# A gated mix of a state-space convolution and an MLP on one core: the front's written order from a re-fitted plan, log dt loaded with the other parameters, the skip term loaded on GpSimd's queue

## The chip, the cores and the metric

One core of one Trainium2 chip. The metric is the device time of one execution in microseconds (us). The kernel before has a median of 525.67 us over 3 runs (524.36 to 526.06). One further execution was profiled; it took 527.21 us, and its span from the first to the last instruction is 525.4 us.

## The reference

Two branches read the same input x (2048 rows by 512 columns, float32), and a gate of each row mixes them:

```python
x = A_u
g = _sigmoid((x * gate_w).sum(-1, keepdims=True))
a = _A_ref(x, A_re, A_im, B_re, B_im, C_re, C_im, log_dt, Dskip)
b = _B_ref(x, w1, b1, w2, b2)          # gelu(x @ w1 + b1) @ w2 + b2, 512 -> 1792 -> 512
return g * a + (1 - g) * b
```

The first branch builds, for each of the 512 channels, a kernel of 2048 taps from 128 complex states, and convolves the channel with it; it then adds the skip term:

```python
P = jnp.exp(logdA[:, :, None] * l[None, None, :])      # logdA = exp(log_dt) * (A_re + i A_im)
K = jnp.einsum("dn,dnl,dn->dl", Cc, P, dB).real
y = irfft(rfft(u, 2L) * rfft(K, 2L))[:L] + u * Dskip
```

## The kernel before, in words

The kernel has two parts. `front` makes the taps, the first stage of the transforms of taps and signal, and nearly all of the MLP. `conv` does the rest of the transforms, the last MLP products and the mix. In the profile, the front fills TensorE until 412.35 us, and the first matmul of `conv` starts at 416.61 us.

**The MLP in the front.** The hidden layer is cut into 64 steps `i`: 16 blocks `b` (8 blocks of 256 rows, each passed twice, with one half of the 1792 hidden columns per pass) times 4 column groups `j`. Every float32 product is made of three matmuls, of a rounded high part and a rest: `xh`, `xlo` for x, `wh`, `wl` for the weights, `hh`, `hl` for the hidden values. A step is `hidden` (L950 to L952, 12 matmuls for each of one or two column tiles, into one of three PSUM buffers `ph`), a gelu and a rounded copy on ScalarE (L967, L970), the rest `hl` on VectorE (L980), and `output` (L998 to L1000, into `acc0` and `acc1`). After j = 3 ScalarE scales `acc` by the gate into `io` (L1019), which SyncE stores in the first pass and GpSimd's queue adds to the output in HBM in the second (L1030).

**The weights.** All of the first half of w1 and w2 is loaded at the start (L1044, 14 loads of 256 KB on SyncE's queue), rounded by ScalarE (`wh`, L828; a few on VectorE, L826) and subtracted on VectorE (`wl`, L830). TensorE runs 13 matmuls on a zeroed tile `dm` before the first weights come (L1055).

**The taps.** 16 chunks, four to each of 4 units of 128 channels. A chunk makes complex powers on VectorE (`cmul`, L534 to L537), magnitudes (L691) and rotations (L703, L710, L714) into `y`, and contracts them over the 128 states on TensorE (`contract`, L728, 128 small matmuls into `pk`). After each second chunk a first stage of the transform follows (`first_stage`, L435, into `ph`, `pk`, `pu0`, `pu1`); ScalarE copies it to `sk` (L754). After each unit, eight transfers on SyncE's queue store `sk` to HBM (`tk_d`, L769). The step sizes dt = exp(log dt) are made once for unit 0 (`first_dt`: an own load of 64 KB, log dt broadcast over the partitions, L515; ten VectorE operations L490 to L503, one Exp L507), and for the other units in `other_dts`. Unit 0's parameters come in another load (`prm`, L556).

**The signal.** In 8 stages, two 128-row tiles of x are loaded (L449) and taken through a first stage (L435). ScalarE copies the four PSUM buffers to three rotating buffers `st` (L453), and two transfers each store them to HBM (`tu_d`, L456). With three buffers for four copies, the fourth copy of a stage (out of `pu1`) waits until the first buffer's two stores have landed.

**What sets the order.** Nothing is written out by hand. Each operation of the front is added to a `Plan` with an engine, an assumed duration (`hold`, in `vec`, `act`, `mm`, `move`), what it reads and writes, and a due time worked out of a table of constants (`T_0`, `LAG`, `D_LO` and so on). `Plan.run` is a small list scheduler: again and again it takes the engine that can start first, and on it the ready operation with the least due time (plus `TABLE` where ScalarE would have to load another function table). Transfers are held to share one wire, and the time of a transfer is its size over a rate of 360 KB per us. The instructions are then issued in the order that comes out, and every engine works its own list strictly in that order. So the constants and the assumed durations act on the chip only through the order. In `conv` the order is written in loops.

Of the kernel before, what the change touches and what calls it, by code (L numbers as in the profile page):

```python
# [32 lines left out]
NB = 2 * NSB  # L33
T_0 = 21.909
T_MLP = 406.545
K_0 = 31.523
T_KG = 356.763
U_0 = 28
U_GAP = 18
LAG = 12.856  # L40
TABLE = 19.14
D_KA = -33.555
D_KP = -84.187
D_S1 = 23.678
D_EV = -33.402
D_H = -65.365
D_LO = -21.589
PS = (2, 3, 1, 2)
N_ACC, N_H, N_PK, N_PU = PS
D_SP = 2.869  # L50
MEM = (6, 2, 3)
N_LD, N_HL, N_ST = MEM
D_XS = -168.313
D_G = 1.725
N_WARM = 13
T_EARLY, T_LOFT, T_DEN = 405.144, 330.334, 535.529
Y_K, Y_U = 43.23, 26.971
W_MLP = (-0.0644, -0.031, 0.0179)
W_KG = (-0.0422, -0.0319, -0.0259)
W_U = (-0.0349, -0.1398, -0.0169)  # L60
D_MAG = -0.166
D_ROT = 0.588
D_CON = 0.043
D_PHA = 0.289
D_PRE = -2.671
D_XL = 25
D_COE = -3.439
D_OUT = -2.679
N_REST = 3
D_KA0 = 0  # L70
D_DT = 19
D_PRM = -248.822
D_D0 = -601.022
D_WAVE0 = -266.408
D_COE0 = -24.094
D_SP1 = -464.705
D_G0 = 1
D_GW = 522.519
D_XS0 = 74.778
T_PRE = 0  # L80
W_CAST = (0, 0, 0, 0, 0, 0, 0, 0, 1, 1, 0, 1, 0, 0)
X_CAST = (1, 0, 1, 0)
D_X0, D_B2, D_B2C = -1509.465, -139.804, -674.499
B_CAST = 1
# [110 lines left out]
LANES = 8  # L195
TURN_PE = 0.095


# [21 lines left out]
class Plan:  # L220
# [26 lines left out]
    def run(self, fixed=None):  # L247
# [13 lines left out]
        for _ in self.tasks:  # L261
# [44 lines left out]
def gated_mix(  # L306
# [6 lines left out]
    logdt: bass.AP,  # L313
    logdt0: bass.AP,
    dskip: bass.AP,
# [33 lines left out]
    def front(pool, psum, keep, attic, loft, den):  # L349
# [133 lines left out]

        def make_dt(x, k, r, ki, key, due, load, store):
# [20 lines left out]
            move(180 if n < UW else 84, load, due - 1, [], [key], hold=0.65 if n < UW else 0.4)  # L505
            vec(4 * (n + 130), before, due, [], [key])
            act(n, lambda: nc.scalar.activation(r, r, AF.Exp, scale=0.25), due, [], [key], table="exp")  # L507
            vec(6 * (n + 130), behind, due, [], [key] if store is r else [key, "dtb"])

        def first_dt():  # L510

            x, k, r, ki = (loft[:, 2048 + UW * m : 2048 + UW * m + UW] for m in range(4))
            make_dt(
                x, k, r, ki.bitcast(I32), "tt", D_D0,
                lambda: nc.sync.dma_start(x, logdt0), dtb,  # L515
            )

        def other_dts():

            x, k, r, ki = dts  # L520
            shape = "o (p c) -> (o p) c"
            make_dt(
                x, k, r, ki.bitcast(I32), "dt", D_DT,
                lambda: nc.sync.dma_start(x, logdt.rearrange(shape, c=4)), r,
            )
            move(180, lambda: nc.sync.dma_start(dt_d.rearrange(shape, c=4), r), D_DT, ["dt"], ["dt_d"], out=True, hold=0.65)

# [23 lines left out]
        def prepare(u, t, eb_k):  # L551
# [3 lines left out]
            act_due = t + D_KA + (0 if u else D_KA0)  # L555
            move(393, lambda: nc.sync.dma_start(pr, prm[u]), t - 20 if u else D_PRM, [], ["pr"])  # L556
            if u:
                move(
                    66, lambda: nc.gpsimd.dma_start(dtb, dt_d[:, sl].to_broadcast([P, UW])), t - 20,
                    ["dt_d"], ["dtb"], queue="GP",  # L560
                )
# [86 lines left out]
        def waves(t):  # L648
# [4 lines left out]

            act(99 * CW, sines, t + D_KA, ["ph"], ["tt"], "sin", ops=3)

# [62 lines left out]
        def contract(u, c, k, t):  # L718
# [45 lines left out]
            for h in range(8):  # L764
# [8 lines left out]

                move(448, store, t + 5, [("sk", i, j) for i in range(2) for j in range(4)], [], out=True, hold=0.65)

# [92 lines left out]
        def dots(b, t):  # L868

            for n in range(2 * b, 2 * b + 2):  # L870
                xd, key = load(xs[n], t - 10)
                vec(
                    512,
                    lambda n=n, xd=xd: nc.vector.scalar_tensor_tensor(
                        xd, xd, 1.0, gwb, ALU.mult, ALU.mult, accum_out=gs[:, n : n + 1]
                    ),
                    t, ["gwb"], [key, ("gs", n // 2)],
                )

        def gates(b0, b1_, t):  # L880
# [11 lines left out]
            )  # L892
            vec(100, sides, t + D_LO, [], keys)

# [45 lines left out]
        def hidden(i, t):  # L940
# [24 lines left out]
            def gelu():  # L965
# [18 lines left out]
        def output(i, t):  # L984
# [19 lines left out]
            for s in range(2):  # L1004
                if b == NB - 1 or i == 4 * NB - 6:
# [5 lines left out]
                mm(  # L1011
                    0.2295 * n, lambda s=s, q=q: products(s, acc[q]), t + LAG + D_OUT * (j == 3),
                    [hk, lk, "b2", *ws], [("acc", q)], lat=0.45,
# [20 lines left out]
        def dense():  # L1034
# [304 lines left out]
_NAMES = [  # L1339
    "xl", "xs", "xt", "prm", "logdt", "logdt0", "dskip", "w1", "b1", "w2", "b2", "gw", "c1", "g1", "c2",  # L1340
]


def layout(inputs):
# [11 lines left out]
    names = ["A_A_re", "A_A_im", "A_B_re", "A_B_im", "A_C_re", "A_C_im"]  # L1356
    prm = np.stack([np.asarray(inputs[n])[order].T for n in names], 1)
    prm = prm.reshape(P, 6, D // UW, UW).transpose(2, 0, 1, 3)
    w1 = np.asarray(inputs["B_w1"]).reshape(4, P, NF, P).transpose(2, 1, 0, 3).reshape(NF, P, D)
# [6 lines left out]
        "logdt": np.asarray(inputs["A_log_dt"])[order].reshape(1, D),  # L1366
        "logdt0": np.broadcast_to(np.asarray(inputs["A_log_dt"])[order][:UW], (P, UW)),
        "dskip": np.asarray(inputs["A_Dskip"])[order].reshape(16, 4, 8).transpose(1, 0, 2).reshape(4, P),
# [34 lines left out]
```

## Time and profile before

| what | value |
|---|---|
| median of 3 runs | 525.67 us (524.36 to 526.06) |
| profiled execution | 527.21 us, span 525.4 us |
| mean granted TensorE clock | 0.986 |
| TensorE busy | 504.2 us (96%) |
| VectorE busy | 428.7 us (82%) |
| ScalarE busy | 351.5 us (67%) |
| GpSimd busy | 42.1 us (8%) |
| moved by DMA | 107.87 MB, 205 GB/s on average |

The busy time of TensorE is an upper bound of its work, since matmuls overlap; where the engine waits is better read from the idle time before single matmuls. A row of the chain of waits gives the start, the length and the engine with its tile and line; "SPq" is SyncE's queue, and "ACT L967" without a tile is the load of a function table. Times in the table of stages are those of one stretch, and "PEclk" is the granted TensorE clock in it.

### The profile page before, as it was taken

How to read it: one execution, taken by the hardware profiler on the slowest of the kernel's cores; microseconds unless marked ns; L12 is line 12 of the kernel's file. 1: busy time of each engine (PE TensorE's matmuls, PEld its weight loads, DVE VectorE, ACT ScalarE, POOL GpSimd, SP SyncE). 2: the span in 40 equal slices, each digit the busy share in tenths (PEclk: the TensorE clock that was granted, in tenths of full speed). 3: DMA queues.
4: the chain of work that ended last, by engine and by line, in shares of the span. 5: the costliest groups of instructions: out<-in, count | busy, mean ns of one | idle time of the engine just before them, and what ended most of it. 6: DMA issues, size and time to landing. Idle time of an engine off the chain costs nothing.

```text
span 525.4 us, 12205 instructions
## 1 busy us (share of the span) xinstructions
PE 504.2 (96%) x4810; PEld 387.0 (74%) x4810; DVE 428.7 (82%) x793; ACT 351.5 (67%) x626; POOL 42.1 (8%) x81
## 2 busy tenths in 40 slices
PE   6999998999999999999999999899999699999995
PEld 6897887799888989888898887778889542222451
DVE  6899989999999997979999899599931177777643
ACT  5798754899884789885686996556644346565311
POOL 2000000000000000002000020001010000110113
PEclk8899999999999999999999999999999899999999
DMA  8867784251684233538462267782388978999978
GB/s 293 327 226 235 262 297 145 81 203 51 186 223 141 81 110 125 193 128 192 91 203 42 81 161 198 165 301 42 113 234 197 291 252 319 354 346 388 343 285 310
DMA packets 80128, 107.87 MB, mean 205 GB/s; under 512 B 39396, under 2 KB 40680, under 8 KB 79528
## 3 DMA queue, kind: packets, MB, share of 16 engines
q1 hardware_dynamic: 74056, 85.10, 50.1%
q0 software_dynamic: 5088, 18.59, 13.3%
q10 hardware_dynamic: 928, 3.41, 1.8%
q8 instruction: 38, 0.62, 0.5%
q14 instruction: 18, 0.15, 0.1%
HBM read 61.46 MB, written 45.62 MB: 204 GB/s over the span
## 4 chain that ended last, share of the span: by engine, by line
PE 72%; ACT 8%; DMA 8%; DVE 8%; SPq 2%; issue 1%; ACTq 0%; DVEq 0%
PE pk L728 9%; PE ph L950 7%; PE ph L952 7%; PE ph L951 7%; PE acc L998 7%; PE acc L999 6%; PE acc L1000 6%; PE p2u L1160 6%; PE p2k L1160 6%; PE pa L1199 3%; DMA tu_d<-attic 3%; PE pb L1304 3%; PE ph L435 2%; DMA attic<-in_xs_dram 2%; SPq L769 2%; ACT ph L967 2%
## 5 line engine op out<-in xcount | busy, mean ns | idle before, releaser
L950 PE MATMUL ph<-xh,wh 128*128 128x256 f32 x448 | 129.2, 288 | 2.2 <-ACT wh L828 2.0
L952 PE MATMUL ph<-xh,wl 128*128 128x256 f32 x448 | 128.2, 286 | 1.2 <-DVE wl L830 1.2
L951 PE MATMUL ph<-xlo,wh 128*128 128x256 f32 x448 | 127.9, 286 | 0.0
L950 PEld LDWEIGHTS ph<-xh,wh 128*128 128x128 f32 x448 | 86.4, 193 | 9.9 <-issue 5.4
L951 PEld LDWEIGHTS ph<-xlo,wh 128*128 128x128 f32 x448 | 86.5, 193 | 2.1
L952 PEld LDWEIGHTS ph<-xh,wl 128*128 128x128 f32 x448 | 86.5, 193 | 1.4 <-DVE wl L830 1.4
L998 PE MATMUL acc<-wh,hh 128*128 128x512 f32 x206 | 82.8, 402 | 2.3 <-ACT hh L970 2.3
L1000 PE MATMUL acc<-wh,hl 128*128 128x512 f32 x206 | 80.9, 393 | 0.5 <-DVE hl L980 0.5
L999 PE MATMUL acc<-wl,hh 128*128 128x512 f32 x206 | 80.9, 393 | 0.0
L967 ACT ACTIVATE ph<-ph,b1t 128x256 f32<-128x256 f32 x112 | 50.4, 450 | 43.2 <-PE ph L952 41.3
L728 PE MATMUL pk<-y,den 128*32 128x64 f32 x2048 | 61.6, 290 | 1.2 <-DVE y L714 1.2
L728 PEld LDWEIGHTS pk<-y,den 128*32 128x32 f32 x2048 | 57.2, 136 | 5.5 <-issue 3.5
L980 DVE TENSOR_TENSOR hl<-ph,hh 128x512 fp32r<-128x512 f32 (+1 forms) x62 | 38.2, 618 | 25.3 <-ACT hh L970 24.9
L998 PEld LDWEIGHTS acc<-wh,hh 128*128 128x128 f32 x206 | 38.7, 188 | 17.5 <-issue 7.2
L691 DVE TENSOR_TENSOR y<-y,ea 128x64 f32<-128x64 f32 (+4 forms) x80 | 45.3, 566 | 3.5 <-ACT y L681 3.0
L1000 PEld LDWEIGHTS acc<-wh,hl 128*128 128x128 f32 x206 | 38.7, 188 | 10.3 <-DVE hl L980 1.6
L999 PEld LDWEIGHTS acc<-wl,hh 128*128 128x128 f32 x206 | 38.7, 188 | 6.3
L534 DVE TENSOR_TENSOR loft<-den,zz 128x256 f32<-128x256 f32 (+2 forms) x48 | 37.3, 777 | 1.1 <-ACT den L660 0.6
L970 ACT CAST hh<-ph 128x512 fp32r<-128x512 f32 (+1 forms) x62 | 33.0, 533 | 7.3 <-PE acc L999 5.5
L1168 ACT COPY k<-p2k 128x512 f32<-128x512 f32 x32 | 18.8, 586 | 28.6 <-issue 13.1
L535 DVE TENSOR_TENSOR loft<-den,zz 128x256 f32<-128x256 f32 (+2 forms) x48 | 37.1, 773 | 0.0
L703 DVE TENSOR_TENSOR y<-y,loft 128x2048 f32<-128x2048 f32 x16 | 36.6, 2285 | 0.0
(193 smaller groups left out, 880.1 us busy)
## 6 DMA issues: line engine op xcount, KB each, us to landing
tu_d<-attic SPq DMA_DIRECT2D x64, 128.0 KB, 3.5
tk_d<-sk SPq DMA_DIRECT2D x32, 256.0 KB, 4.9
t_d<-sa SPq DMA_DIRECT2D x32, 256.0 KB, 5.1
tk<-tk_d SPq DMA_DIRECT2D x24, 256.0 KB, 4.9
t<-t_d POOLq DMA_DIRECT2D x9, 512.0 KB, 6.4
attic<-in_xt_dram SPq DMA_DIRECT2D x16, 256.0 KB, 4.5
attic<-in_xs_dram SPq DMA_DIRECT2D x16, 256.0 KB, 4.9
xh_d<-xh SPq DMA_DIRECT2D x8, 512.0 KB, 3.8
```

The lines of the kernel that those rows point to most:

```text
L534: vec(2 * m, lambda: vv.tensor_mul(t, a, br), due, [ka, *kb], [kt])
L691: nc.vector.tensor_mul(both(n, 64 - 3 * n, n), both(0, 64 - n, n), an)
L728: nc.tensor.matmul(pks[q][32 * j : 32 * j + 32, :, gg], x[:, r, :, ch], y[:, r, :, ch], start=(r == 0), stop=(r == 1), skip_group_check=True,)
L950: nc.tensor.matmul(p, h, xh[xk][:, d], start=(d == 0), stop=False)
L951: nc.tensor.matmul(p, h, xlo[xk][:, d], start=False, stop=False)
L952: nc.tensor.matmul(p, lo, xh[xk][:, d], start=False, stop=(d == 3))
L967: nc.scalar.activation(phs[q][:, n], phs[q][:, n], AF.Gelu_apprx_tanh, bias=b1t[:, f : f + 1])
L980: nc.vector.tensor_sub(lo, phs[q][:, 0:nf], hi.bitcast(F32))
L998: nc.tensor.matmul(a, h, wh[1][w], start=start, stop=False)
L999: nc.tensor.matmul(a, h, wl[1][w], start=False, stop=False)
L1000: nc.tensor.matmul(a, l, wh[1][w], start=False, stop=(j == 3))
L1160: nc.tensor.matmul(out[64 * i : 64 * i + 64], w, x, start=True, stop=True)
```

## The change

Five things are changed, and lines after the first of them move by one to four.

1. **The planner's costs.** In `Plan.run` every transfer that starts after 22 us takes 1.18 times as long on the wire. The ScalarE cost of the gelu step and of the sines, and the VectorE cost of the gate's products, are raised; the broadcast of dt counts 300 KB where it counted 66 KB. Nearly all due times have new values, and the output products of the block before the last get an offset of their own (`D_LAST`).
2. **log dt beside the parameters.** The tile `pr` has seven slices where it had six, and the seventh is what was the tile `dtb`. For unit 0 one load brings all seven (448 KB); the load of 64 KB and its input are gone. Units 1 to 3 load six slices, and GpSimd's queue loads dt into the seventh, as before.
3. **The skip term.** Its load of 2 KB into `dm` moves from SyncE's queue to GpSimd's.
4. **Both halves of the first x block** are rounded by ScalarE (`X_CAST`); one was rounded by VectorE.
5. **The order** that follows from the plan.

```diff
-T_0 = 21.909
-T_MLP = 406.545
+T_0 = 22.399
+T_MLP = 408.145
...
-LAG = 12.856
-TABLE = 19.14
+LAG = 14.812
+TABLE = 27.405
...
+D_LAST = -1.557
...
-X_CAST = (1, 0, 1, 0)
+X_CAST = (0, 0, 1, 0)
...
+SLOW = 1.18
...
-                wire = max(wire, at + before) + took
+                wire = max(wire, at + before) + took * (SLOW if at > 22.0 else 1.0)
...
-        pr = pool.tile([P, 6, UW], F32, name="pr")
-        dtb = pool.tile([P, UW], F32, name="dtb")
+        pr = pool.tile([P, 7, UW], F32, name="pr")
+        dtb = pr[:, 6]
...
-            x, k, r, ki = (loft[:, 2048 + UW * m : 2048 + UW * m + UW] for m in range(4))
-            make_dt(
-                x, k, r, ki.bitcast(I32), "tt", D_D0,
-                lambda: nc.sync.dma_start(x, logdt0), dtb,
-            )
+            k, r, ki = (loft[:, 2048 + UW * m : 2048 + UW * m + UW] for m in range(3))
+            move(459, lambda: nc.sync.dma_start(pr, prm[0]), D_PRM, [], ["pr", "dtb"])
+            make_dt(dtb, k, r, ki.bitcast(I32), ["tt", "dtb"], D_D0, dtb)
...
-            move(393, lambda: nc.sync.dma_start(pr, prm[u]), t - 20 if u else D_PRM, [], ["pr"])
             if u:
+                move(393, lambda: nc.sync.dma_start(pr[:, 0:6], prm[u, :, 0:6]), t - 20, [], ["pr"])
...
-                ops=nf + 2,
+                ops=nf + 3.3,
...
-                    mm(0.2295 * n, ..., t + LAG + D_OUT * (j == 3),
+                    mm(0.2295 * n, ..., t + LAG + D_OUT * (j == 3) + D_LAST * (b == NB - 2) * j,
...
-            move(20, lambda: nc.sync.dma_start(dm[0:P:32], dskip), -80, [], ["dm"], hold=0.65)
+            pl.add("GP", 0.7, lambda: nc.gpsimd.dma_start(dm[0:P:32], dskip), D_DM, [], ["dm"], wire=(0.2, (2.2, 9.0)))
```

The order moves on every engine, while the number and the shapes of the operations stay the same but for the load and the cast named. Three places matter below.

**VectorE, at the start.** Before, from the second half of x's rest (`xlo`) on; L498 to L503 are the second part of dt's chain, and `wl00` is the first weight tile's rest, without which the first column tile's third matmul can't run:

```order
L830 TENSOR_TENSOR xlo00_108<-attic_76,xh00_106 128x512
L498 TENSOR_TENSOR loft_77<-loft_77 128x128
L499 TENSOR_TENSOR loft_77<-loft_77 128x128
L500 TENSOR_SCALAR loft_77<-loft_77 128x128
L501 TENSOR_SCALAR loft_77<-loft_77 128x128
L502 CAST loft_77<-loft_77 128x128
L503 TENSOR_TENSOR dtb_101<-loft_77 128x128
L830 TENSOR_TENSOR wl00_124<-sk_93,wh00_110 128x512
```

The same place now:

```order
L826 TENSOR_TENSOR xlo00_107<-attic_76,xh00_105 128x512 x2
L491 TENSOR_SCALAR loft_77<-pr_100 128x128
L492 TENSOR_SCALAR loft_77<-loft_77 128x128
L493 SCALAR_TENSOR_TENSOR loft_77<-loft_77,pr_100 128x128
L494 SCALAR_TENSOR_TENSOR loft_77<-loft_77 128x128
L826 TENSOR_TENSOR wl00_123<-sk_93,wh00_109 128x512
L499 TENSOR_TENSOR loft_77<-loft_77 128x128
```

Both halves of `xlo` now stand ahead of the whole dt chain, and `wl00` stands between its first four and its last six operations. On ScalarE the Exp of that chain (L507) stood ahead of the first weight cast (`wh00`), and now stands behind it.

**ScalarE, at the eighth and last signal stage** (near 337 us in the profile). Before, from the scaled outputs of a block on; L650 to L652 are the sines of the next chunk of taps, L453 the fourth copy of the signal stage, L967 and L970 gelu and rounded copy of a hidden step, L660 and L681 copies that the next chunk needs:

```order
L1019 ACTIVATE io0_144<-acc0_85,gate_69 128x512
L1019 ACTIVATE io1_145<-acc1_86,gate_69 128x512
L650 ACTIVATE loft_77<-phase_95 128x1056
L651 ACT_TABLE_LOAD
L651 ACTIVATE loft_77<-phase_95 128x1056
L652 ACTIVATE loft_77<-loft_77,half_pi_64 128x1056
L453 COPY attic_76<-pu1_92 128x512
L967 ACT_TABLE_LOAD
L967 ACTIVATE ph1_88<-ph1_88,b1t_68 128x256 x2
L970 CAST hh1_139<-ph1_88 128x512
L660 COPY den_78<-x4_97 128x2x128
L681 COPY y_94<-ea1_99 128x32
```

The same place now (L646 to L648 are the sines, L454 the copy, L963 and L966 gelu and copy, L677 and L656 the chunk's copies):

```order
L1016 ACTIVATE io0_143<-acc0_85,gate_69 128x512
L1016 ACTIVATE io1_144<-acc1_86,gate_69 128x512
L646 ACTIVATE loft_77<-phase_95 128x1056
L647 ACT_TABLE_LOAD
L647 ACTIVATE loft_77<-phase_95 128x1056
L648 ACTIVATE loft_77<-loft_77,half_pi_64 128x1056
L963 ACT_TABLE_LOAD
L963 ACTIVATE ph1_88<-ph1_88,b1t_68 128x256 x2
L966 CAST hh1_138<-ph1_88 128x512
L454 COPY attic_76<-pu1_92 128x512
L677 COPY y_94<-ea1_99 128x32
L656 COPY den_78<-x4_97 128x2x128
```

The fourth copy has moved behind the gelu and the rounded copy of `hh1`. It still stands ahead of the two copies for the next chunk. At the second and the sixth stage it has moved behind a gelu in the same way, at the third behind sines, and at the fourth behind the next chunk's copies.

**ScalarE, at the last first stage of the taps** (394 us in the profile). Before; L746 is a copy of the contraction, L754 are the four copies to `sk`:

```order
L967 ACTIVATE ph0_87<-ph0_87,b1t_68 128x256 x2
L970 CAST hh1_139<-ph0_87 128x512
L746 COPY s11_105<-pk0_90 128x512
L967 ACTIVATE ph1_88<-ph1_88,b1t_68 128x256 x2
L970 CAST hh2_140<-ph1_88 128x512
L754 COPY sk_93<-ph0_87 128x64x8
L754 COPY sk_93<-pk0_90 128x64x8
L754 COPY sk_93<-pu0_91 128x64x8
L754 COPY sk_93<-pu1_92 128x64x8
L967 ACTIVATE ph2_89<-ph2_89,b1t_68 128x256
L970 CAST hh1_139<-ph2_89 128x256
```

The same place now:

```order
L742 COPY s11_104<-pk0_90 128x512
L963 ACTIVATE ph0_87<-ph0_87,b1t_68 128x256 x2
L966 CAST hh1_138<-ph0_87 128x512
L750 COPY sk_93<-ph2_89 128x64x8
L750 COPY sk_93<-pk0_90 128x64x8
L750 COPY sk_93<-pu0_91 128x64x8
L750 COPY sk_93<-pu1_92 128x64x8
L963 ACTIVATE ph1_88<-ph1_88,b1t_68 128x256 x2
L966 CAST hh2_139<-ph1_88 128x512
L963 ACTIVATE ph2_89<-ph2_89,b1t_68 128x256
L966 CAST hh1_138<-ph2_89 128x256
```

One hidden step of two column tiles (`ph1`, 24 matmuls on TensorE) stood ahead of the four copies and now stands behind them. On TensorE, between the last matmul of that first stage and the first matmul of `conv`, there were 96 hidden and 30 output matmuls, and now there are 120 and 30. On SyncE's queue, between the last eight stores to `tk_d` and the constants and taps that `conv` loads first, there were two loads of the signal, and now there are three.

More of the change, by code (lines that the diff above doesn't have):

```diff
@@ L33 @@
 NB = 2 * NSB
-T_0 = 21.909
-T_MLP = 406.545
-K_0 = 31.523
-T_KG = 356.763
-U_0 = 28
-U_GAP = 18
-LAG = 12.856
-TABLE = 19.14
[L42 to L47, printed above, removed]
+T_0 = 22.399
+T_MLP = 408.145
+K_0 = 32.114
+T_KG = 351.806
+U_0 = 29
+U_GAP = 18
+LAG = 14.812
+TABLE = 27.405
+D_KA = -32.407
+D_KP = -80.929
+D_S1 = 7.912
+D_EV = -40.921
+D_H = -80.673
+D_LO = -23.342
 PS = (2, 3, 1, 2)
 N_ACC, N_H, N_PK, N_PU = PS
-D_SP = 2.869
+D_SP = -0.52
 MEM = (6, 2, 3)
 N_LD, N_HL, N_ST = MEM
-D_XS = -168.313
-D_G = 1.725
+D_XS = -157.526
+D_G = 1.227
 N_WARM = 13
-T_EARLY, T_LOFT, T_DEN = 405.144, 330.334, 535.529
-Y_K, Y_U = 43.23, 26.971
+T_EARLY, T_LOFT, T_DEN = 353.026, 381.686, 484.328
+Y_K, Y_U = 44.535, 26.725
 W_MLP = (-0.0644, -0.031, 0.0179)
[L59 to L68, printed above, removed]
+W_KG = (-0.0372, -0.0319, -0.0262)
+W_U = (-0.0347, -0.139, -0.0186)
+D_MAG = -0.783
+D_ROT = 0.578
+D_CON = 0.705
+D_PHA = 0.305
+D_PRE = -3.087
+D_XL = 34
+D_COE = -3.192
+D_OUT = -3.305
+D_LAST = -1.557
 N_REST = 3
 D_KA0 = 0
[L71 to L79, printed above, removed]
+D_DT = 5
+D_PRM = -277.043
+D_D0 = -1024.07
+D_WAVE0 = -343.734
+D_COE0 = -66.219
+D_SP1 = -461.8
+D_G0 = 2
+D_GW = 598.738
+D_XS0 = 98.527
 T_PRE = 0
 W_CAST = (0, 0, 0, 0, 0, 0, 0, 0, 1, 1, 0, 1, 0, 0)
-X_CAST = (1, 0, 1, 0)
-D_X0, D_B2, D_B2C = -1509.465, -139.804, -674.499
+X_CAST = (0, 0, 1, 0)
+D_X0, D_B2, D_B2C, D_DM = -1313.069, -235.635, -950.754, -4.033
 B_CAST = 1
@@ L481, in early, with make_dt @@
             yield None
-        def make_dt(x, k, r, ki, key, due, load, store):
+        def make_dt(x, k, r, ki, keys, due, store):
             ln2h = 355.0 / 512.0
@@ L503, in behind @@
                 v.tensor_mul(store, r, ki.bitcast(F32))
[L505 to L508, printed above, removed]
+            vec(4 * (n + 130), before, due, [], keys)
+            act(n, lambda: nc.scalar.activation(r, r, AF.Exp, scale=0.25), due, [], keys[:1], table="exp")
+            vec(6 * (n + 130), behind, due, [], keys)
         def first_dt():
-            x, k, r, ki = (loft[:, 2048 + UW * m : 2048 + UW * m + UW] for m in range(4))
-            make_dt(
-                x, k, r, ki.bitcast(I32), "tt", D_D0,
-                lambda: nc.sync.dma_start(x, logdt0), dtb,
-            )
+            k, r, ki = (loft[:, 2048 + UW * m : 2048 + UW * m + UW] for m in range(3))
+            move(459, lambda: nc.sync.dma_start(pr, prm[0]), D_PRM, [], ["pr", "dtb"])
+            make_dt(dtb, k, r, ki.bitcast(I32), ["tt", "dtb"], D_D0, dtb)
         def other_dts():
@@ L772, in store @@
                     )
-                move(448, store, t + 5, [("sk", i, j) for i in range(2) for j in range(4)], [], out=True, hold=0.65)
+                move(450, store, t + 5, [("sk", i, j) for i in range(2) for j in range(4)], [], out=True, hold=0.65)
         def taps():
@@ L1011, in output @@
                 mm(
-                    0.2295 * n, lambda s=s, q=q: products(s, acc[q]), t + LAG + D_OUT * (j == 3),
+                    0.2295 * n, lambda s=s, q=q: products(s, acc[q]),
+                    t + LAG + D_OUT * (j == 3) + D_LAST * (b == NB - 2) * j,
                     [hk, lk, "b2", *ws], [("acc", q)], lat=0.45,
@@ L1356, in layout @@
     names = ["A_A_re", "A_A_im", "A_B_re", "A_B_im", "A_C_re", "A_C_im"]
-    prm = np.stack([np.asarray(inputs[n])[order].T for n in names], 1)
-    prm = prm.reshape(P, 6, D // UW, UW).transpose(2, 0, 1, 3)
+    prm = [np.asarray(inputs[n])[order].T for n in names]
+    prm.append(np.broadcast_to(np.asarray(inputs["A_log_dt"])[order], (P, D)))
+    prm = np.stack(prm, 1).reshape(P, 7, D // UW, UW).transpose(2, 0, 1, 3)
     w1 = np.asarray(inputs["B_w1"]).reshape(4, P, NF, P).transpose(2, 1, 0, 3).reshape(NF, P, D)
```

18 lines of the change are left out of this document (7 added, 11 removed).

## The prediction

> **What bounds the kernel now.** I read the stages first, with the busy time of each engine in them. The first number of a row is its length; then come TensorE, its weight loads, VectorE, ScalarE and GpSimd, the granted clock, the share of DMA, and GB/s.
>
> ```profile
> 20.90:385.10 364.20, 357.13 (x3914) 307.69 (x3912) 339.92 (x642) 278.74 (x493) 22.20 (x46) 1.00 0.55 162
> 385.10:412.40 27.30, 27.25 (x301) 24.50 (x299) 3.37 (x6) 11.86 (x25) 2.46 (x3) 1.00 0.83 179
> 412.40:421.90 9.50, 5.29 (x13) 3.00 (x15) 1.12 (x2) 2.81 (x7) 0.00 (x0) 0.64 1.02 358
> ```
>
> TensorE has work nearly all the time, so a new order can only win back what TensorE waits, and what it does at half clock. From 20.9 to 385.1 us VectorE is busy for 339.92 of 364.20 us as well (93%). So the two are bound together there: what VectorE loses soon reaches TensorE. Then the waits of TensorE (total, times, longest):
>
> ```profile
> PE p2k L1160 <- DMA tk<-tk_d: 4.3, 1, 4.3
> PE acc L998 <- ACT hh L970: 2.3, 1, 2.3
> PE ph L435 <- DVE hl L980: 2.1, 1, 2.1
> PE ph L950 <- ACT wh L828: 2.0, 1, 2.0
> PE pk L728 <- DVE y L714: 1.2, 1, 1.2
> PE ph L952 <- DVE wl L830: 1.2, 1, 1.2
> ```
>
> These are 13.1 us in all, in four places: the start (2.0 and 1.2), one near 80 us (2.1), a stall near 340 us (2.3, and then 1.2), and the passage from the front to `conv` (4.3). All that the change can bring lies in these, in what follows from the clock, and in new waits of its own. `conv` is written in loops and isn't touched; I take it as it is, but for its clock at the beginning.
>
> **Part 1, the start.** The chain of waits shows how dt stands in the way:
>
> ```profile
> 1.67 4.33 DMA loft<-in_logdt_dram
> ...
> 9.19 0.70 DVE wl L830
> 9.89 0.04 issue
> 9.93 0.58 PE ph L952
> ```
>
> VectorE waits until 6.0 us for log dt, then makes the first part of dt, the second half of x's rest and the six last operations of dt, and only at 9.19 us the first weight's rest, on which the third matmul waits. ScalarE's first weight casts:
>
> ```profile
> 7.60 4.72 ACT L828 CAST wh<-sk 128x512 fp32r<-128x512 f32 x7
> ```
>
> Seven take 4.72 us, 0.67 each, so `wh00` is there at 7.60 + 0.67 = 8.3 us. Now `wl00` comes right after it and takes 0.70: TensorE's third matmul starts at 9.0 us where it was 9.93, a gain of 0.9. That the load of log dt leaves SyncE's queue can only bring the first weight sooner. The other side: the six operations of dt are only moved behind, so VectorE has the same sum of work ahead of the later weights, but for one cast. Bounds: 0 (the later weight rests set the pace again) and 2.0 (the other wait of the start goes too, as if the first weight came that much sooner); I take 0.8, nearer to the row of the 1.2 wait than to nothing.
>
> The skip term's load is one issue on either queue. On GpSimd it waits for the 13 first matmuls to end, since they read `dm`, and behind it stand a memset of `y` and the loads of dt for units 1 to 3, the first of them here:
>
> ```profile
> 27.38 0.58 POOL L559 DMA_DIRECT2D dtb<-dt_d  x1 [23.16 <-DVE xh L826]
> ```
>
> GpSimd was idle for 23.16 us before it, and this idle time covers the wait; so I cost it at nothing. With that cover gone, the load of dt for unit 1 would come later by what is over. The zeroing of `dm`, now behind four other memsets, starts the first matmuls a little later; they then end nearer to the first weights, which can only help the clock.
>
> **Part 2, the stall near 337 us.** The chain of waits, by start and length:
>
> ```profile
> 330.03 7.29 DMA tu_d<-attic
> 337.36 0.04 issue
> 337.40 0.59 ACT attic L453
> 338.00 1.28 ACT L967
> 339.30 0.46 ACT ph L967
> 339.78 0.46 ACT ph L967
> 340.26 0.59 ACT hh L970
> ```
>
> The fourth copy of the signal stage waits for two stores of the first buffer, which stand in line behind the eight stores to `tk_d`. Behind the copy, ScalarE holds the gelu and `hh`, on which TensorE (2.3) and VectorE wait. The waits of ScalarE and VectorE at such places:
>
> ```profile
> ACT attic L453 <- DMA tu_d<-attic: 11.6, 7, 5.0
> DVE hl L980 <- ACT hh L970: 24.9, 15, 5.6
> ```
>
> The 5.0 and the 5.6 are those of this place. In the new order table load, gelu and `hh` (1.28 + 0.46 + 0.46 + 0.59 = 2.8 us) stand ahead of the copy, and nothing that they need hangs on it. They fill ScalarE's wait, so `hh` comes some 5 us sooner, and the 2.3 of TensorE go. VectorE then has most of its 5.6 us back; about 1 us of it stays, since the copies for the next chunk still stand behind the fourth copy. What is late next is the chunk's `y` (the wait of 1.2 at L714), and it is late because VectorE was; with 4 us more in hand it goes too. Sum: 2.3 + 1.2 = 3.5. Bounds: 1.2 (the stores land still later) to 5.6 (all 2.1 near 80 us, of the same kind but for VectorE's load, goes too).
>
> **Part 3, the passage to `conv`.**
>
> ```profile
> 391.38 0.12 PE ph L951
> ...
> 394.27 1.97 ACT sk L754 x4
> ...
> 404.75 5.21 DMA tk_d<-sk
> ...
> 410.04 6.44 DMA tk<-tk_d
> 416.48 0.14 issue
> 416.61 4.25 PE p2k L1160 x8
> 420.86 2.32 PE p2u L1160 x8
> 423.18 1.72 PE p2k L1160 x8
> ```
>
> From the four copies on, the chain is fixed: 416.48 - 394.27 = 22.2 us. TensorE covers it with the hidden and output matmuls that are left. One step of 24 matmuls has moved from ahead of the last first stage to behind it, at 0.12 us each: 24 x 0.12 = 2.9 us more cover. Against it, one more load of 256 KB stands ahead of the first taps; at the 358 GB/s that the row of 412.4 to 421.9 us shows, 262,144 bytes take 0.73 us. So the wait of 4.3 becomes 4.3 - 2.9 + 0.7 = 2.1, a gain of 2.2. Bounds: 0 (transfers that now meet lengthen the chain by another 2.2) to 4.3. The step must be there in time: the last chunk's contraction now comes 2.9 us sooner against TensorE's end, which takes VectorE's time from part 2.
>
> **Part 4, the clock.** Four stretches along the changes of the granted clock:
>
> ```profile
> 5.52:8.93 3.41, 1.28 (x9) 0.89 (x8) 2.71 (x10) 1.55 (x3) 0.00 (x0) 1.00 0.94 333
> 8.93:15.76 6.83, 5.83 (x27) 5.83 (x28) 6.73 (x15) 5.08 (x8) 0.00 (x0) 0.50 1.05 383
> 411.70:415.12 3.42, 0.65 (x6) 0.45 (x4) 1.12 (x2) 1.49 (x4) 0.00 (x0) 1.00 1.06 309
> 415.12:421.95 6.83, 5.34 (x13) 3.05 (x15) 0.00 (x0) 1.99 (x4) 0.00 (x0) 0.50 1.01 371
> ```
>
> Twice a stretch of 3.4 us with little work (1.28 and 0.65 us) is followed by 6.83 us at half clock. In the second, 416.61 to 421.95 = 5.34 us of `conv` run at half speed, which costs 5.34 / 2 = 2.7. The wait of 2.3 near 338 us, by contrast, left the clock at 1.00. So with a wait of 2.1 I take the 2.7 as gone. On this the Trainium skill, "TensorE: Matmul & The Clock Gate", section "HAM oscillation — how this bites in real kernels", has a rule: idle gaps of TensorE should stay under about 3.4 us. By that rule alone 2.1 us are safe and the 2.7 are won. The first row speaks against taking it as the whole story: there 1.28 us of 3.41 were busy, no gap was longer than 2.0, and the clock was halved. By that row a wait of 2.1 that falls into one stretch whole leaves 1.3 busy, and nothing is won; this is a rival below.
>
> **New waits.** The new order is as tight as the old one, and it will miss somewhere too. I price one miss of the size of the wait near 80 us: +2.1, with bounds 0 and 4.
>
> **The sum.** -0.8 - 3.5 - 2.2 - 2.7 + 2.1 = -7.1. Against the profiled execution's 527.21 us this gives 520.1; that execution was 1.5 us above the median of the three runs, 525.67, on which the forecast stands: 525.67 - 7.1 = 518.6. With the bounds on the good side (-2.0, -5.6, -4.3, -2.7, 0) it would be 511.1, with those on the other (0, -1.2, 0, 0, +4) 528.5. Not all fall together; this case's own range is 513.5 to 522.5.
>
> **Rivals.**
>
> *The wait moves to VectorE (slower).* The seven waits of the fourth copy make 11.6 us, and only their place in ScalarE's list has changed. At the last stage the two copies for the next chunk still stand behind it. If the taps wait at each stage as TensorE did at one, the 3.5 of part 2 aren't won, and 11.6 - 5.0 = 6.6 us that other work hid come on top: -7.1 + 3.5 + 6.6 = +3.0, 528.7 us. For it speaks that VectorE has only 24 us of slack in 364; against it, that at the fourth stage the chunk's copies have moved ahead of the copy. It decides from 3.6 us of those 6.6 on.
>
> *The passage stays as it is.* The three loads and the two adds to the output on GpSimd's queue now lie closer to the first taps, and the chain grows by what the cover grew. Neither 2.2 nor 2.7 is won: -2.2, 523.5 us. DMA is at 1.02 of its capacity there, which speaks for it.
>
> *The clock is halved all the same.* The wait is 2.1, but falls into one 3.4 us stretch: -4.4, 521.3 us. Its start must lie in the first 1.3 of 3.4 us, about 4 in 10; and the row of 1.28 busy us must hold for such a stretch, which the wait near 338 us leaves open.
>
> *The plan's gain doesn't carry to the chip.* Old waits go and as many new ones come, in the front and at the passage: 525.7 us. The order was already made by a plan of this kind, which didn't see these waits.
>
> **The numbers.** Forecast 0.50, clock 0.14, passage 0.13, no gain 0.10, VectorE 0.13. The likeliest gives 518.6 us. For 8 in 10 the range goes from 513.5 to 526.0: left out are the slower rival, a few hundredths below, and a few above from the case without gain. A measurement of this kernel tells about 0.3% (1.6 us) from no change. Faster by more than that: the forecast, the clock, and two thirds of the passage, with little of the rest: 0.75. Within it: most of the case without gain and a third of the passage, 0.12. Slower: 0.13.
>
> **What would show it.** In the profile after: the third matmul of the MLP at about 9 us; no wait of TensorE on `hh` near 337 us, and the fourth copy still idle there for some us; a last wait on `tk` of about 2 us, and a granted clock of 1.00 behind it, so that the first eight matmuls of `conv` take about 1.7 us and not 4.25. The prediction is wrong if the wait on `tk` is still over 4 us, if VectorE's idle time between 20 and 385 us grows beyond 24 us, or if TensorE shows new waits of more than 4 us in sum.

## The result, and the profile after

The changed kernel takes 520.32 us, the median of 17 runs (517.59 to 524.80). The kernel before, measured beside it, takes 527.88 us (17 runs, 524.36 to 533.24). The ratio is 0.9858, with a 95% interval from 0.9829 to 0.9888. On the 525.67 us on which the forecast of 518.6 stands, this ratio is 518.2 us: 7.5 us won (5.9 to 9.0), where 7.1 were forecast. The profiled execution took 517.95 us, with a span of 515.7 and a mean clock of 0.995. It lies at the fast end of its runs, so the two profiled executions are 9.3 us apart, and the two traces explain a little more than the medians show.

First the waits of TensorE after (total, times, longest):

```profile
PE ph L946 <- DVE hl L976: 2.9, 2, 1.8
PE pk L1052 <- POOL dm L1047: 2.2, 1, 2.2
PE ph L948 <- DVE wl L826: 1.4, 4, 0.6
PE acc L996 <- DVE hl L976: 0.8, 1, 0.8
PE acc L989 <- ACT io L1016: 0.4, 1, 0.4
PE ph L946 <- ACT wh L824: 0.3, 1, 0.3
```

The 4.3 on `tk`, the 2.3 on `hh`, the 1.2 on `y` and the 2.1 near 80 us are gone. What is new is the wait on `hl`, in three places: 1.8 us at 19.5, 1.1 near 303 and 0.8 at 342. The 2.2 on `dm` stand at the very start, where nothing can run anyway.

Next VectorE from 20 to 385 us, before and after (the third number with a bracket):

```profile
20.00:385.00 365.00, 357.93 (x3921) 308.50 (x3920) 340.37 (x642) 279.63 (x494) 22.09 (x46) 1.00 0.55 163
```

```profile
20.00:385.00 365.00, 361.04 (x4037) 312.41 (x4038) 340.05 (x644) 276.48 (x492) 22.88 (x46) 1.00 0.57 166
```

VectorE is busy for the same 340 us of these 365, while TensorE works 3.1 us more. So VectorE's waits have moved and not grown (24.6 us idle before, 25.0 after). At the last signal stage this can be read from the chain of waits:

```profile
330.50 6.52 DMA tu_d<-attic
...
337.10 0.58 ACT attic L454
337.69 0.13 ACT y L677
```

and from two waits of VectorE:

```profile
DVE hl L976 <- ACT hh L966: 19.1, 12, 4.2
DVE y L687 <- ACT y L677: 3.3, 2, 3.0
```

The fourth copy still waits for the two stores, but `hh` is no longer behind it: VectorE's longest wait on `hh` was 5.6 and is 4.2 (at the end of the front, where TensorE doesn't need it), and 3.0 of the old 5.6 stay with the next chunk's `y`.

At the passage, SyncE's queue issues the last stores, three loads of the signal, a constant and the first two taps:

```profile
395.48 3.50 SPq L765 DMA_DIRECT2D tk_d<-sk  x3
399.02 1.37 SPq L479 DMA_DIRECT2D loft<-tu_d  x1
400.49 1.23 SPq L479 DMA_DIRECT2D den<-tu_d  x2
401.82 0.38 SPq L1130 DMA_DIRECT2D cc<-in_c_dram  x1
402.37 0.79 SPq L1138 DMA_DIRECT2D tk<-tk_d  x2
```

The first tap lands at 408.42 us, and the first matmul of `conv` starts at 408.51, right behind the last hidden one. From there to the first inverse matmul (L1199 before, L1196 after) it took 11.65 us before, at a mean granted clock of 0.77, and takes 9.88 at 1.00:

```profile
416.61:428.26 11.65, 11.65 (x40) 6.31 (x40) 5.84 (x10) 3.79 (x8) 0.00 (x0) 0.77 0.78 269
```

```profile
408.51:418.39 9.88, 9.77 (x41) 5.06 (x40) 6.96 (x12) 5.44 (x12) 0.00 (x0) 1.00 1.07 361
```

To see where the time went although the orders differ, I counted for each kernel what TensorE has lost by a given time: the time, less the matmuls issued by then at the usual distance of their kind in these traces (0.120 us for a hidden one, 0.234 output, 0.066 first stage, 0.029 contraction, 0.228 and 0.127 in `conv`). The rows below the first two are the experiments.

```
lost by (us)    28    60   140   320   380   440
before        13.0  14.3  18.6  20.5  25.5  32.4
after         14.4  15.5  16.5  20.0  21.7  22.6
b_fill        11.6  12.9  18.3  20.5  27.1  32.4
b_copy        11.4  12.6  16.9  19.2  21.4  28.2
b_dot         11.4  12.6  18.8  20.7  28.2  34.7
b_all3        11.1  12.4  19.5  21.4  22.8  27.3
b_lateadd     11.7  13.0  17.9  19.9  25.5  29.6
a_nocover     14.0  15.0  16.0  19.7  21.2  28.6
a_start       12.1  15.5  16.5  20.2  22.3  23.1
a_slow1       12.5  15.4  17.4  20.9  22.7  24.4
a_oldstart    12.3  15.5  16.5  20.2  21.2  23.1
a_best        12.1  15.6  16.7  19.7  22.2  24.0
a_best2       11.6  14.9  15.9  19.2  21.4  23.1
a_best3       12.1  15.4  16.5  19.7  21.4  22.6
```

From one column to the next, after against before: -2.1 by 140 us, +1.6 from there to 320, -3.3 from 320 to 380, -6.0 from 380 to 440, and nothing after that (less than 0.2). That is -9.8, and the spans differ by 9.7. By 320 us all fourteen kernels have lost 19.2 to 21.4 us, whatever their start and whatever they had won by 140 us. So what tells the two kernels apart comes almost wholly behind that time.

### The profile page after: what moved, and what is told of

Its sections match the earlier page's. It is cut to its first block, busy times and chain, and to the rows that moved or that the text cites. A ratio compares the mean times of both kernels' runs of the same rounds, so it can differ in the third digit from the quotient of the medians.

```text
span 515.7 us, 12196 instructions
## 1 busy us (share of the span) xinstructions
PE 501.5 (97%) x4810; PEld 385.1 (75%) x4810; DVE 427.5 (83%) x792; ACT 349.6 (68%) x625; POOL 42.6 (8%) x82
## 3 DMA queue, kind: packets, MB, share of 16 engines
q10 hardware_dynamic: 928, 3.41, 1.8%
## 4 chain that ended last, share of the span: by engine, by line
PE 79%; ACT 7%; DVE 7%; DMA 4%; issue 1%; SPq 1%; DVEq 0%; ACTq 0%
PE pk L724 10%; PE ph L946 8%; PE acc L994 8%; PE ph L948 8%; PE ph L947 8%; PE acc L996 7%; PE acc L995 7%; PE p2u L1157 6%; PE p2k L1157 5%; PE pa L1196 3%; PE pb L1301 3%; PE ph L436 3%; DMA tk<-tk_d 1%; DMA tu_d<-attic 1%; DMA sk<-in_w_dram 1%
## 5 line engine op out<-in xcount | busy, mean ns | idle before, releaser
L963 ACT ACTIVATE ph<-ph,b1t 128x256 f32<-128x256 f32 x112 | 50.5, 451 | 39.2 <-PE ph L948 37.4
L976 DVE TENSOR_TENSOR hl<-ph,hh 128x512 fp32r<-128x512 f32 (+1 forms) x62 | 38.1, 616 | 19.2 <-ACT hh L966 19.1
L966 ACT CAST hh<-ph 128x512 fp32r<-128x512 f32 (+1 forms) x62 | 33.0, 532 | 13.6 <-PE acc L995 12.0
```

Source lines behind the costliest of these rows:

```text
L963: nc.scalar.activation(phs[q][:, n], phs[q][:, n], AF.Gelu_apprx_tanh, bias=b1t[:, f : f + 1])
L976: nc.vector.tensor_sub(lo, phs[q][:, 0:nf], hi.bitcast(F32))
```

## The experiments

Twelve kernels were run. Names with b are the kernel before, with a the changed kernel, each with the edit shown. Ratios are against the kernel before, measured in the same series; the change alone has 0.9858. In most of them the order comes from the plan, and single entries are then moved (or, in b_fill, added) by hand, so that nothing else changes; a_slow1 is planned anew, and in a_oldstart and a_best2 the lists behind the start are fixed to the changed kernel's. The diffs show the engine's list.

**b_fill: work in the wait on `tk`.**

```diff
 TensorE, end of the front
 hidden ph0, last 12 matmuls
+14 products of the zeroed tile, 128x128
 conv: p2k<-tk
```

> The kernel before, with 14 products of the zeroed tile on TensorE between its last hidden matmul and the first matmul of conv (some 3.0 us at 0.213 each, inside the wait of 4.3 on tk); nothing else moves, and the products are used by nobody. The forecast's step on the clock: a stretch with little work is what halves it, so with 3.0 us of work in the wait the granted clock stays at 1.00 behind it, and 2.7 us are won; the changed kernel's trace gives less for the same stretch (first conv matmul to first inverse matmul 11.65 before, 9.88 after, 1.8 us). So -1.8 to -2.7, a ratio of 0.995 to 0.9966, with the wait of 4.3 cut to about 1.3 and the first conv matmul where it was. Rival: the clock falls there for another reason (the full DMA queues, the change of shape), then 6.83 us at 0.50 stand behind the wait as before and the ratio is 1.000.

Measured: 0.9947 (0.9920 to 0.9974), -2.8 us. The stretch from the first `conv` matmul to the first inverse one runs at full clock:

```profile
418.93:428.23 9.30, 9.30 (x40) 5.03 (x40) 5.84 (x10) 3.80 (x8) 0.00 (x0) 1.00 0.89 312
```

9.30 us against 11.65. The wait is cut from 4.3 us, about as far as expected:

```profile
PE p2k L1164 <- DMA tk<-tk_d: 1.8, 1, 1.8
```

The first `conv` matmul comes later than before in this trace, which had lost 1.6 us more by 380 us. Work that nobody uses, put into the wait, holds the clock: what halves it is that TensorE has little to do.

**b_copy: the fourth copy alone.**

```diff
 ScalarE, last signal stage
-COPY attic<-pu1
 ACT_TABLE_LOAD
 ACTIVATE ph1 x2
 CAST hh1
+COPY attic<-pu1
```

> The kernel before, with one entry moved on ScalarE: the fourth signal copy of the last stage goes behind the gelu and the rounded copy that stood behind it. Forecast: the wait of 2.3 on hh near 338 us goes and the 1.2 on y near 351 us with it, -3.5, ratio 0.9934. Rival 1: only the 2.3 go, since the next chunk's two copies still stand behind the fourth copy and VectorE stays as late as it was: 0.9956. Rival 2: VectorE's wait moves the stall to the taps and TensorE waits as long there: 1.000 or above.

Measured: 0.9930 (0.9901 to 0.9959), -3.7 us. From 320 to 380 us TensorE loses 2.2 us where it lost 5.0, and in other traces with the old place up to 7.5. So the forecast's step of 3.5 holds with one entry moved. The wait on `hh` is gone, but the wait on `y` is not:

```profile
PE pk L728 <- DVE y L714: 1.1, 1, 1.1
```

Over all traces the place of this copy parts the kernels: between 320 and 380 us TensorE loses 5.0 to 7.5 us in the four with the old place, and 1.0 to 2.5 in the ten with the new one.

**b_dot: the gate product near 75 us alone.**

```diff
 VectorE, near 75 us
-gate product, second x tile (waits 1.77 us for its load)
 ... 11 entries, among them hl 128x512 and hl 128x256
+gate product, second x tile
```

> The kernel before, with one entry moved on VectorE: the second gate product near 75 us, which waited 1.77 us for its load of x, goes behind the second rest hl that stood 11 entries later. The forecast had no step for this place (it priced the 2.1 only as a bound). New theory: that load came later than the plan thought, and the 1.77 us of VectorE are the 2.1 us of TensorE at 79.9 us: -2.1, ratio 0.996. Rival: VectorE is 93% busy, so what is won here is lost at the next place where hl is late, and the ratio is 0.999 to 1.000.

Measured: 1.0000 (0.9969 to 1.0032). The rival holds. The wait of 2.1 is gone, and from 72 to 140 us these two stand in its place:

```profile
PE ph L435 <- ACT s L746: 1.4, 1, 1.4
PE acc L993 <- ACT io L1019: 0.9, 1, 0.9
```

By 140 us the kernel has lost 18.8 us, as before. One entry doesn't win what the whole new order wins there.

**b_all3: the three edits at once.**

```diff
+the 14 products of b_fill
+the moved copy of b_copy
+the moved gate product of b_dot
```

> The kernel before with the three edits of the other runs at once: the copy, the gate product, the filled wait. If they add up: -3.5 -2.1 -1.8 = -7.4, ratio 0.986, as much as the whole change. If the stalls stand for one another (VectorE sets the pace in the front), the first two give no more than the larger of them: -3.5 -1.8 = -5.3, 0.990, or less.

Measured: 0.9895 (0.9855 to 0.9934), -5.5 us. The product of the three single ratios is 0.9877, inside the interval, so they add up as far as this can be told. Two entries and a filler, then, win about three quarters of the change by the medians; the interval allows for half of it to all.

**a_nocover: the hidden step back ahead of the last first stage.**

```diff
 TensorE                          ScalarE
+hidden ph1, 24 matmuls          +gelu ph1 x2, hh2
 last first stage of the taps     four copies to sk
-hidden ph1, 24 matmuls          -gelu ph1 x2, hh2
```

> The changed kernel with one hidden step (24 matmuls, its gelu and its rounded copy) put back ahead of the last first stage of the taps and its four copies, where the kernel before had it. The forecast's step: 2.9 us of cover for the chain of stores and loads. In the changed kernel tk lands 0.09 us before the first conv matmul, so a wait of 2.8 on tk comes back: +2.8 against the changed kernel, and +1.8 more if the clock is halved behind it; ratio against the kernel before 0.991 with the clock at 1.00, 0.9946 with it halved. Rival: the wait went because the eight stores and the loads moved faster in the new order, not by the cover; then under 1.5 us come back, ratio 0.9885 or less.

Measured: 0.9963 (0.9939 to 0.9988), 5.5 us worse than the change. The wait that comes back is larger than the cover that was taken away:

```profile
PE p2k L1171 <- DMA tk<-tk_d: 5.1, 1, 5.1
```

and the clock is halved for 6.83 us behind it. From the last first stage to the landing of `tk` it takes 24.3 us here, and 22.0 in the changed kernel. So the step did more than cover 2.9 us: with it, that way also became shorter. Three loads of the signal stand ahead of the first tap here as in the changed kernel, so the number of loads is not what makes the way long.

**b_lateadd: the two adds to the output, later.**

```diff
 ScalarE, end of the front
-ACTIVATE io0<-acc0, io1<-acc1
 ACTIVATE ph1 x2
 CAST xh00
+ACTIVATE io0<-acc0, io1<-acc1
```

> The kernel before with one thing moved on ScalarE at the end of the front: the two scaled outputs, on which GpSimd's two adds to the output wait, go behind the next gelu and rounded copy, so that the adds are issued some 4 us later, close to the first load of tk as in the changed kernel. Theory: the adds, issued 2 to 6 us ahead of that load in every kernel with the old tail and within 0.7 us of it with the new one, are what makes the way from the last first stage to the landing of tk 23.3 to 24.5 us long there and 22.0 to 23.3 here. So it becomes some 22.5 us, the wait on tk falls from about 4.6 to 3.3, ratio 0.9975 (and 0.994 if the clock then stays up). Rival: that way varies for other reasons, stays at 23.3 or more, and the ratio is 1.000.

Measured: 0.9909 (0.9875 to 0.9944), -4.8 us, more than either figure that was expected; its trace has 2.8 of it (4.1 us lost from 380 to 440 us, 6.9 before), and the rest stays open. GpSimd's adds in this kernel, and in the kernel before:

```profile
410.48 1.72 POOL L1030 DMA_DIRECT2D out_dram<-io  x2 [24.67 <-ACT io L1019]
```

```profile
406.24 1.72 POOL L1030 DMA_DIRECT2D out_dram<-io  x2 [20.39 <-ACT io L1019]
```

The first tap's load, issued at 409.10 us, is now ahead of them:

```profile
404.79 4.23 DMA tk_d<-sk
...
409.10 5.37 DMA tk<-tk_d
...
414.60 2.78 PE p2k L1174 x7
```

The last store lands after 4.23 us where it took 5.21, the load after 5.37 where it took 6.44, and the whole way falls from 23.3 to 21.4 us. In the changed kernel the adds are issued at 402.40, the load at 402.37. With the old tail they came 3 to 6 us ahead of it in every other trace. A second pair of traces shows the same: with the adds later, a_best3 has a way of 21.4 us, where a_best has 23.3. The Trainium skill, "DMA: Bandwidth & Descriptors", section "Queues, rings and completion order", says that a DMA engine takes turns between the queues that have work for it. No trace here shows the turns themselves; what these traces show is that the last store and the first load on SyncE's queue are each about 1 us longer where the adds are issued ahead of that load.

**a_start: output matmuls first.**

```diff
 TensorE, near 20 us
-hidden ph0, 12 matmuls (waits 1.77 us on hl)
 output acc0, acc1, 7 matmuls each
+hidden ph0, 12 matmuls
```

> The changed kernel with 12 hidden matmuls (the fourth column tile's step) moved behind the first two groups of output matmuls, as the kernel before had them. Theory: the start lost its lead there. These 12 wait 1.77 us at 19.6 for hl, the stretch of 3.41 us holds 1.64 us of work, and the next one runs at half clock. With output matmuls first, some 0.5 to 0.7 us of work fill the wait and the clock stays at 1.00: -0.5 from the wait and -1.5 from the clock, about -2, ratio against the kernel before 0.982 (the change alone 0.9858). Rival: the clock is halved all the same, and VectorE's hl sets the pace as it did: -0.5 or nothing, 0.985 to 0.986.

Measured: 0.9856 (0.9823 to 0.9890). The clock stayed at 1.00, as the theory has it, but its 2 us aren't there: by 28 us the kernel has lost 2.3 us less than the changed one; by 60 us it has lost the same 15.5.

**a_oldstart: the start as it was before.**

```diff
+log dt in its own load; skip term on SyncE's queue; one half of x rounded on VectorE
+VectorE: dt chain, then wl00         ScalarE: Exp, then wh00         GpSimd: dm zeroed first
 (behind the start, every list is the changed kernel's)
```

> The changed kernel with the start as it was before: log dt in its own load of 64 KB, the skip term on SyncE's queue behind the weights, one half of the first x block rounded on VectorE, dt's chain ahead of the first weight rest, and dm zeroed first. The order is pinned: behind the start every engine's list is that of the changed kernel. Theory: the forecast's -0.8 for the start came from one execution in which log dt landed late (5.99 us); in four later executions with the old start it landed at 4.6 to 5.4, and there TensorE is 1.4 to 1.9 us ahead at 32 us of where it is with the new start. So the old start wins some 1.6 us: ratio against the kernel before 0.983, hl at about 20.0 us on VectorE where it was 20.7. Rival 1, the forecast's step: the new start is worth 0.8, and the ratio is 0.9875. Rival 2: the lead is lost to VectorE by 100 us, and the ratio is 0.9858, that of the change.

Measured: 0.9863 (0.9822 to 0.9903). The start, old or new, is worth nothing that can be measured here. The interval alone would allow for the theory (0.983) and for rival 1 (0.9875) as well; for rival 2 speak the traces. By 28 us this kernel is ahead, and then VectorE waits for a load of x:

```profile
25.82 0.43 DVE L828 CAST xh<-attic 128x512 fp32r<-128x512 f32 x1 [2.07 <-DMA attic<-in_xt_dram]
```

By 60 us it has lost 15.5 us, like the others.

**a_slow1: the plan's factor for transfers back at 1.0.**

```diff
-SLOW = 1.18
+SLOW = 1.0
```

> The changed kernel with the plan's factor for transfers after 22 us at 1.0 instead of 1.18; all due times and other costs stay. In the order that moves three of the fourth signal copies by two to four places on ScalarE, one gate product near 75 us and three other pairs on VectorE, and some transfers; TensorE's list stays. Theory: the factor is what put the gate product behind its load, so VectorE waits some 1.8 us there again and TensorE about 2 near 80 us: +2, ratio against the kernel before 0.990. Rival: the due times had already done it, and the factor is worth nothing measurable: 0.986.

Measured: 0.9844 (0.9811 to 0.9877). The theory's 0.990 lies outside the interval, and the rival holds. With the new due times kept, the factor itself is worth nothing measurable.

**a_best, a_best2, a_best3: can more be had?** a_best takes a_start and moves two rests `hl` ahead of a long operation; a_best2 does the same on the old start; a_best3 is a_best with the later adds of b_lateadd.

```diff
 VectorE, near 303 and 342 us
+hl<-ph,hh
 rotation 128x1024 (303 us); magnitude and phase 128x1024 (342 us)
-hl<-ph,hh
```

> The changed kernel with the edit at the start and two more, on VectorE: the rests hl near 304 and 342 us, on which TensorE waits 1.15 and 0.80, go ahead of the long rotation and the long magnitude in front of them. If each wait goes and nothing takes its place: -2.0 -0.8 -0.9 = -3.7 against the changed kernel, ratio against the kernel before 0.979. Rival: VectorE's work is only moved, and the taps make TensorE wait as much a little later: -2 at most, 0.982.

> The same old start, pinned, with the three moves of the run that had output matmuls first and two rests hl earlier on VectorE. If the start is worth 1.6 and the moves what they showed there (0.9838 against 0.9858, about 1): ratio against the kernel before 0.981. Rival: the moves were noise, and it is that of the old start alone, 0.983; second rival: neither is worth anything, 0.9858.

> The changed kernel with the three moves of the run at 0.9838 and, besides, the two scaled outputs moved behind the next gelu and rounded copy at the end of the front, as in the run on the kernel before that gave 0.9909. There the way from the last first stage to the landing of tk fell from 23.3 to 21.4 us. TensorE covers 22.0 us of it here, so what is left of the wait, 0 to 1.3 us in the traces of this family (mean 0.6), goes, and no more: -0.6 against the run at 0.9838, ratio against the kernel before 0.9825, with no wait on tk in the trace. Rival: the later adds now meet the loads of the following taps, conv waits there for as much, and the ratio is 0.984 or above.

Measured: 0.9838 (0.9807 to 0.9868), 0.9875 (0.9831 to 0.9919) and 0.9832 (0.9801 to 0.9863). None can be told from the change, and the 0.979 and 0.981 of the theories of a_best and a_best2 lie outside their intervals. In a_best3 `tk` landed at 407.40, 0.6 us ahead of its matmul, as expected, but from the first `conv` matmul to the first inverse one it took 10.1 us, where it is 9.9 in the changed kernel, so that the rival can't be told from noise.

## Why the prediction was right, step by step

**The start (-0.8): mis-sized, nothing of it can be measured.** The third matmul started at 9.18 us, near the 9.0 of the forecast and ahead of the 9.93 before. But the row on which the step stood, log dt landing at 6.0 us, was one late transfer: in the seven other traces with the old start it landed at 4.6 to 5.4. And what is won there doesn't last. At 28 us the kernels with the new front lie between 11.6 and 14.4 us of loss, at 60 us between 14.9 and 15.6, whatever their start. So the size was the low bound of the step. That the later weight rests set the pace again, as that bound had it, is not shown: where the lead is lost in a_oldstart, VectorE waits for x.

**The stall near 337 us (-3.5): right, for a trace whose clock held.** The traces show -3.3 and the single edit -3.7. The copy's new place is the cause, as forecast. That "about 1 us" of VectorE's wait stays was too little (3.0 stay), and in b_copy the wait on `y` stayed as well; what the stall costs beyond its 2.3 us differs from trace to trace. In b_fill, b_dot and b_lateadd it was 3.1, 4.4 and 3.0 us long, and the clock was halved behind it. The step had no term for that; in the profile that it was read from, the clock held.

**The passage (-2.2): the direction right, one term wrong.** The cover of 2.9 us is there. The 0.7 us that I charged for one more load ahead of `tk` do not show: these loads are issued while the last stores are still under way, and `tk` has to wait for the last store to land. What I had down as a rival, the adds on GpSimd's queue, is the real other term, with the opposite sign. Since the outputs come later against the last first stage, the adds now meet the first loads of the taps rather than the last stores. The way to `tk` was 23.3 to 24.5 us in the six traces with the old tail and the adds at their old place; it is 22.0 to 23.3 in the traces with the new tail (without a_best3, whose adds come later). So about 1.2 us are won (between the means) where 0.7 were charged, and of the wait of 4.3 there remain 0 to 1.3 us, not 2.1.

**The clock (-2.7): the mechanism right, the size between 1.8 and 2.8.** The single edit gives -2.8 (1.4 to 4.2). In the traces the stretch is 1.8 us shorter after, and 2.3 in b_fill, since the changed kernel waits a little for the second tap and the first constants: its first eight matmuls took 3.1 us, not the 1.7 that I expected. The rival, a halved clock behind a wait of about 2 us, didn't happen because the wait was smaller, but its mechanism is real. In b_lateadd the wait was 2.3, and:

```profile
412.39:415.80 3.41, 1.20 (x5) 0.66 (x7) 1.11 (x2) 1.62 (x5) 0.00 (x0) 1.00 1.03 233
415.80:419.22 3.42, 3.42 (x11) 1.83 (x8) 0.00 (x0) 1.17 (x2) 0.00 (x0) 0.50 1.08 319
```

**New waits (+2.1): near in size, by luck.** The new waits on `hl` are 1.8, 1.1 and 0.8 us, but no place for them was named, and two of the three lie at the start and at the stall. From 140 to 320 us the loss grew by 1.6, which is about what had been won by 140 us.

**What was not a step: the stretch from 60 to 140 us.** There the kernel before loses 4.3 us and the changed one 1.0. I had the 2.1 at 80 us only as a bound. In the five b traces the loss there is 4.3 to 7.1 us, and in each the clock is halved once, at 81 to 100 us; in the eight traces of the changed kernel and its variants it is 1.0 to 2.0, and the clock holds. But by 320 us this gain is gone again. Which of the moves there does it stays open: b_dot shows that the gate product alone doesn't, and a_slow1 that the factor for transfers isn't needed once the due times are as they are.

**The sum.** Up to 320 us the forecast had -0.8 and +2.1, together +1.3, and the traces have -0.5, within what they differ by. For the stall it had -3.5 (traces -3.3), for the passage with the clock -4.9 (traces -6.0). So the two steps that make the gain stood on the right mechanisms, while it is luck that the misses elsewhere nearly cancel. Of the signs of being wrong, VectorE's idle time was set at 24 us, where it stood already; it grew by 0.3. The new waits on `hl` make 3.7 us, just under the 4 that was set; with the longer wait on `dm` at the start (2.2 us, before 1.0) they would be over it.

The rival on the slower side, that the waits of the fourth copies move to VectorE, is refuted by the same 340 us of work in 365: its waits were moved, not added.

## What to carry to other kernels

In this kernel, where two engines are bound together, what is won in the first 140 us is lost again by 320 us, while the stall near 337 us and the wait at the passage, which nothing makes up for, are worth their full length or more. At such a passage look at all queues: here adds that weren't needed yet, issued some 4 us later, shortened the way to the first tap by about 2 us. And don't price a step from one late transfer of one trace.

## What the runs showed of the hardware

TensorE's granted clock changes on a grid of 3.41 us, whose position differs from run to run. Over the fourteen traces, counting the stretches that lie whole in the span, 26 stretches of the grid at full clock were followed by half clock: TensorE was busy in them for 0 to 2.07 us. The 2034 that were followed by full clock had 1.53 or more. At half clock, 5 with up to 2.80 us of busy time were followed by half clock again, and 23 with 2.96 or more by full. So it is the share of work in a stretch that counts: about half of it at full clock, over four fifths at half clock. Between 1.53 and 2.07 us both happened. In the changed kernel a single wait of 1.8 us at the start was enough:

```profile
18.54:21.95 3.41, 1.64 (x14) 1.47 (x13) 3.41 (x8) 1.71 (x2) 0.00 (x0) 1.00 1.04 409
21.95:25.37 3.42, 3.42 (x15) 3.13 (x14) 2.75 (x15) 1.20 (x6) 0.00 (x0) 0.50 0.67 244
```

a_slow1 has the same list at the start and the same wait, its grid fell otherwise (2.15 us busy in the stretch from 20.13 us), and the clock stayed:

```profile
20.13:23.54 3.41, 2.15 (x15) 2.10 (x16) 3.24 (x12) 0.26 (x2) 0.00 (x0) 1.00 1.01 394
```

The Trainium skill, "TensorE: Matmul & The Clock Gate", section "HAM oscillation — how this bites in real kernels", asks for no idle gap over about 3.4 us. Here gaps of 1.8 and 2.3 us halved the clock, so the measurement decides: what has to be kept is work in about half of every 3.4 us.
